# The first key piece as three transfers by partition modulo 4, and two small loads on GpSimd's queue

## The chip, the cores and the metric

The kernel runs on one core of one Trainium2 chip. The metric is the device time of one execution in microseconds (us), and the figure compared is the median over runs. Times inside an execution are counted from the start of the profiled span.

## The reference

One decode step for two sequences. A row `x` of 448 numbers per sequence is normalised; from it 16 query heads are projected, each attends to the last 4096 positions of a key and value cache (8 key/value heads, 256 wide, two query heads to one key head), and beside that a dense layer with a mish activation works on the same normalised row. The result is the sum of both and of `x`.

```python
def reference(A_x, A_k_cache, A_v_cache, A_wq, A_wo, B_x, B_w1, B_b1, B_w2):
    def _A_ref(x, k_cache, v_cache, wq, wo):
        W = min(4096, max(256, Sk // 4))
        rep = Hq // Hkv
        q = (x @ wq).reshape(B, Sq, Hq, Dh).transpose(0, 2, 1, 3)
        k = jnp.repeat(k_cache[:, :, Sk - W:, :], rep, axis=1)
        v = jnp.repeat(v_cache[:, :, Sk - W:, :], rep, axis=1)
        p = _softmax(jnp.einsum("bhqd,bhkd->bhqk", q, k) * (Dh ** -0.5), axis=-1)
        o = jnp.einsum("bhqk,bhkd->bhqd", p, v)
        return o.transpose(0, 2, 1, 3).reshape(B, Sq, Hq * Dh) @ wo
    def _B_ref(x, w1, b1, w2):
        h = jnp.einsum("bsd,df->bsf", x, w1) + b1
        sp = jnp.log1p(jnp.exp(-jnp.abs(h))) + jnp.where(h > 0, h, 0)
        return jnp.einsum("bsf,fd->bsd", h * jnp.tanh(sp), w2)
    xn = _layernorm(A_x, axis=-1)
    return A_x + _A_ref(xn, A_k_cache, A_v_cache, A_wq, A_wo) + _B_ref(xn, B_w1, B_b1, B_w2)
```

Everything is bf16. The keys and values that are read come to 67 MB, the weights to about 10 MB; the arithmetic on them is small.

## The kernel before

The eight key/value heads of the two sequences are taken in four steps `u` of four (sequence, head) pairs each; such a pair is called `j` below. A step needs two key pieces and two value pieces of 4 MB. All pieces, and the large weights `wq`, `w1` and `w2`, pass through a ring of three buffers of 128 partitions by 32 KB (`ring`, L87). A key piece (`load_k`, L92 to L99, its transfer L98) is laid out with partition p = 4c + j: c counts 32 stretches of the 4096 positions, j the four pairs, and every partition gets one run of 32 KB. So a piece is 128 runs, and all partitions with the same p modulo 4 hold one pair.

A key piece is turned by two VectorE transposes into `kt` (`turns`, L275), multiplied with the queries on TensorE (`scores`, L362), exponentiated on ScalarE (L370) and turned again on VectorE (L373). The value pieces are then multiplied by the weights (`values`, L408). Output projection and dense layer follow in the gaps, and the last step ends in the sum `acc` (L255), its copy to `res` (L626, L628) and the store (L629).

The order of work on every engine is the order in which the program is written, by hand (`tc.manual_schedule()`). SyncE (SP in the profile) issues nearly all transfers. Its queue begins with key piece (0,0) at L98, `wq` at L132 and key piece (0,1) at L98; these three fill the ring. The next issue, `w1` (L506), waits until `turns(0, 0)` has freed the first buffer, the next key piece waits until `project()` (L297) has used `wq`, and so on through the kernel. Ahead of it all ScalarE's queue issues two small loads, `x` (2 rows of 896 bytes, L126) and the bias `b1` (2 rows of 1792 bytes, L128). GpSimd (POOL) issues no transfer; its queue makes the identity matrix and then clears and fills constants: `qd` (L141), `ones`, `hot` (L151, L153), `xs` (L222) and `sp` (L287).

What hangs on `x`: VectorE's statistics (L162, L164), the normalised row (L171), its seven slices (L217), seven small transposes on TensorE (L218) and the copies into `xs` (L226). These stand in VectorE's queue ahead of `turns(0, 0)`, and between them stand constants that don't need `x` (L180 to L205). The bias is read first at L516, in the dense layer.

Of the kernel before, what the change touches and what calls it, by code (L numbers as in the profile page):

```python
# [17 lines left out]
def kernel(  # L18
# [13 lines left out]
    nc = tc.nc  # L32
    P = 128
    G = 4
    J = 4
    R = 4
    RK = 2
# [48 lines left out]
    KE = T * Dh  # L86
# [3 lines left out]
    def ring(name):  # L90
        return kv_pool.tile([P, RK * KE], BF16, tag="kv", name=name)

    k_t, v_t, wo_t = {}, {}, {}

    def load_k(u, r):
        t = ring("k")
        src = kview[u][:, s0:, :].rearrange("j (c t) d -> c j (t d)", c=C)
        nc.sync.dma_start(out=t[:], in_=src[:, :, r * RK * KE : (r + 1) * RK * KE])  # L98
        k_t[u, r] = t  # L99

    def load_v(u, g, lo=0, hi=TV):
# [8 lines left out]
    def load_wo(u):  # L110
# [12 lines left out]
        wo_t[u] = w  # L123

    x_bf = consts.tile([Bsz, D], BF16)
    nc.scalar.dma_start(out=x_bf[:, :], in_=A_x.flatten_outer_dims())  # L126
    b1_sb = consts.tile([2, F2], BF16)
    nc.scalar.dma_start(out=b1_sb[:], in_=B_b1.rearrange("(k f) -> k f", k=2))  # L128

    load_k(0, 0)  # L130
    wq = ring("wq")
    nc.sync.dma_start(  # L132
        out=wq[:, 0 : NS * HW], in_=A_wq.flatten().rearrange("(p e) -> p e", p=P)
    )
    wq_t = [wq[:, i * HW : (i + 1) * HW] for i in range(NS)]
    load_k(0, 1)

    ident = consts.tile([P, P], BF16)
    make_identity(nc, ident[:])
    qd = consts.tile([P, U, 2 * NB, G, NQ], BF16)  # L140
    nc.gpsimd.memset(qd[:], 0.0)  # L141
    ones = consts.tile([P, P], BF16)
# [3 lines left out]
        out=halves[:], in_=ident[0:2, 0:2].unsqueeze(2).to_broadcast([2, 2, Bsz])  # L146
# [5 lines left out]
    for k in range(KU):  # L152
        nc.gpsimd.tensor_copy(  # L153
            out=hot[:, k, :, :, :, k],
            in_=ident[:].rearrange("p (q y) -> p y q", y=4).unsqueeze(2)
# [11 lines left out]
        out=rstd[:], in_=mv[:, 1:2], func=ACT.Sqrt, bias=eps_t[:], scale=1.0  # L167
# [4 lines left out]
        out=xn_bf[:],  # L172
# [8 lines left out]
        out=parm[:], in_=ident[:].rearrange("p (a o) -> p o a", o=2), axis=AXIS.X, op=ALU.add  # L181
# [3 lines left out]
        out=jm[:],  # L185
        in_=ident[:].rearrange("p (a j h) -> p j a h", j=J, h=rep),
# [4 lines left out]
        out=jm[:], in0=jm[:], scalar1=-1.0, scalar2=29952.0, op0=ALU.add, op1=ALU.mult  # L191
# [3 lines left out]
        out=mneg[:], in_=jm[:].unsqueeze(1).to_broadcast([P, TH * 8, J])  # L195
    )
    sel = consts.tile([P, 2, NQ], FP32)
    for x in range(2):
        for w in range(4):
            at = 32 * w + (2 * (w % 2) + x) * NQ  # L200
            src = ident[:, at : at + NQ]
            if w == 0:
                nc.vector.tensor_copy(out=sel[:, x, :], in_=src)
            else:
                nc.vector.tensor_tensor(  # L205
                    out=sel[:, x, :], in0=sel[:, x, :], in1=src, op=ALU.add
# [4 lines left out]
    for s in range(NS):  # L211
        r = s // 2
        step = 3 + s % 2
# [9 lines left out]
    for odd in range(2):  # L223
        for half in range(2):
            o = (half + odd) % 2
            nc.vector.tensor_scalar(  # L226
                out=xs[:, odd::2, half * Bsz : (half + 1) * Bsz],
# [55 lines left out]
    for n in range(2):  # L283
        for e in range(2):
# [3 lines left out]
                out=sp[:],  # L288
                in_=ident[:, o : o + 63 : 2].unsqueeze(1).to_broadcast([P, G, 32]),
# [293 lines left out]
    for u in range(U - 1):  # L583
        load_k(u + 1, 0)
        load_v(u, 0)
        load_k(u + 1, 1)
        load_v(u, 1)
        load_wo(u)
        turns(u + 1, 0)
        values(u, 0)  # L590
        scores(u + 1, 0)
        turns(u + 1, 1)
        values(u, 1)
        gather(u)
        finish(u)
        scores(u + 1, 1)
        relay(u)
        mix_early(u)
        if u < U - 2:
            weigh(u + 1)  # L600
    u = U - 1
# [20 lines left out]
    for g in range(G):  # L622
        dst = res[:, g * DG : (g + 1) * DG]
        src = acc[32 * g : 32 * g + Bsz, :]
# [35 lines left out]
```

## Time and profile before

| what | us |
|---|---|
| median of 4 runs (lowest, highest) | 189.34 (189.28, 189.42) |
| the profiled execution's own time | 189.44 |
| its span in the profile | 187.6 |
| PE, VectorE, ScalarE, GpSimd busy | 74.1, 92.4, 12.4, 4.9 |
| first key piece, from issue to the transpose that waits for it | 0.73 to 13.39 |
| last weight transfer landed, last matmul group starts | 183.79, 183.84 |

The profiled execution is 0.10 us above the median, and 1.84 us of it lie outside the span. Busy times are of one execution; a transfer's row shows when its instruction was issued and how long the issue took, and not when its bytes moved. Stretches ("windows") give the mean busy share of the 16 DMA engines and the rate; a packet's whole time is put into the stretch in which it starts, so that shares over 1 stand next to shares under 1 where the stretches are short.

### The profile page before, as it was taken

Reading aid. Unit: us, or ns where it says so; the run is one execution under the profiler, and the core shown is the slowest. Engines: PE = TensorE matmul, PEld = TensorE weight load, DVE = VectorE, ACT = ScalarE, POOL = GpSimd, SP = SyncE. Lnnn points to the kernel's source line nnn. Section 1 sums busy time; section 2 is a strip of 40 time slices with the busy share of each in tenths; the row PEclk is TensorE's granted clock in tenths of the full one; section 3 lists DMA queues with packets and bytes.
Section 4 is the critical chain, followed back from the end, with each engine's and each line's share of the span. In section 5 each row is a group of like instructions: output and inputs, shape, how many; then the busy total and the mean of one; then the engine's idle time right before and its main releaser. Section 6 shows DMA issues by size and latency. Waiting matters only on the chain.

```text
span 187.6 us, 1952 instructions
## 1 busy us (share of the span) xinstructions
PE 74.1 (40%) x852; PEld 34.5 (18%) x856; DVE 92.4 (49%) x93; ACT 12.4 (7%) x26; POOL 4.9 (3%) x16
## 2 busy tenths in 40 slices
PE   0300367593119000882047002870068005854763
PEld 0100122451003000340012001430022002422452
DVE  6619724984891097038930395048910692040101
ACT  3000030101000100110001000110001000120101
POOL 8100000000000000000000000000000000000000
PEclk9999999999657955699559855798556655899555
DMA  6999999999999999999999999999999999999991
GB/s 225 433 421 428 430 433 406 475 444 433 419 412 430 426 449 387 472 447 433 440 412 409 440 440 418 449 437 447 433 426 412 426 433 433 433 416 398 432 406 40
DMA packets 4451, 77.78 MB, mean 415 GB/s; under 512 B 470, under 2 KB 1244, under 8 KB 2012
## 3 DMA queue, kind: packets, MB, share of 16 engines
q1 hardware_dynamic: 4436, 77.66, 96.8%
q8 instruction: 6, 0.10, 0.2%
q10 hardware_dynamic: 8, 0.01, 0.0%
q14 instruction: 1, 0.01, 0.0%
HBM read 77.67 MB, written 0.00 MB: 414 GB/s over the span
## 4 chain that ended last, share of the span: by engine, by line
DMA 57%; DVE 24%; PE 15%; ACT 2%; issue 1%; another core or an unknown queue 1%; SPq 0%; DVEq 0%
DMA v<-in_A_v_cache_dram 31%; DMA w<-in_B_w_dram 19%; DVE kt L275 19%; DMA k<-in_A_k_cache_dram 7%; PE pv L408 6%; PE sc L362 4%; DVE p L373 2%; PE h_ps L525 2%; PE o L426 1%; DVE rec L394 1%; ACT ex L370 1%; ACT vs L420 1%; PE acc L255 1%; DVE px L342 0%
## 5 line engine op out<-in xcount | busy, mean ns | idle before, releaser
L275 DVE STREAM_TRANSPOSE kt<-k 128x4096 f32<-128x4096 f32 x16 | 70.1, 4418 | 36.5 <-DMA k<-in_A_k_cache_dram 36.5
L408 PE MATMUL pv<-v,p 128*32 128x512 bf16 x240 | 24.3, 574 | 73.7 <-DMA v<-in_A_v_cache_dram 73.7
L408 PEld LDWEIGHTS <-p 128*32 128x32 bf16 x240 | 8.7, 130 | 86.4 <-issue 63.4
L362 PE MATMUL sc<-kt,qd 128*32 128x512 bf16 x256 | 20.1, 457 | 1.8 <-DVE qd L330 1.4
L453 DVE TENSOR_TENSOR oT<-o,rec 128x16 bf16<-128x16 f32 x4 | 0.7, 176 | 23.4 <-PE o L426 19.1
L373 DVE STREAM_TRANSPOSE p<-ex 128x512 bf16<-128x512 bf16 x8 | 5.2, 691 | 10.8 <-ACT ex L370 10.8
L370 ACT ACTIVATE ex<-sc 128x512 bf16<-128x512 f32 x8 | 4.8, 598 | 75.3 <-PE sc L362 75.3
L362 PEld LDWEIGHTS <-qd 128*32 128x32 bf16 x256 | 7.0, 107 | 12.3 <-issue 6.8
L297 PE MATMUL q_ps<-wq,xs 128*32 128x512 bf16 x28 | 3.2, 629 | 13.8 <-DMA wq<-in_A_wq_dram 13.8
L394 DVE TENSOR_REDUCE rec<-dn 128x8 f32<-128x512 f32 x4 | 2.8, 692 | 11.0 <-PE dn L386 9.6
L420 ACT COPY vs<-pv 128x512 f32<-128x512 f32 x4 | 2.3, 586 | 57.2 <-PE pv L408 57.2
L426 PE MATMUL o<-sel,vs 128*128 128x8 f32 x32 | 5.2, 289 | 2.1 <-ACT vs L420 2.1
L426 PEld LDWEIGHTS o<-sel,vs 128*128 128x128 f32 x32 | 4.8, 228 | 5.5 <-ACT vs L420 5.5
L487 PE MATMUL early<-wo,ox 128*2 128x448 bf16 x24 | 5.0, 352 | 1.9 <-ACT ox L478 1.9
L525 PE MATMUL h_ps<-xs,w 128*128 128x4 bf16 x49 | 3.7, 196 | 2.3 <-DMA w<-in_B_w_dram 2.3
L297 PEld LDWEIGHTS <-xs 128*32 128x32 bf16 x28 | 1.1, 136 | 15.5 <-issue 15.5
L386 PE MATMUL dn<-p,ones 128*128 128x512 bf16 x5 | 2.0, 433 | 4.1 <-DVE p L344 3.8
L218 PE MATMUL xr_ps<-ident,xrows 2*128 2x2 bf16 x7 | 1.0, 182 | 6.7 <-DVE xrows L217 6.7
L525 PEld LDWEIGHTS <-w 128*128 128x128 bf16 x49 | 3.2, 150 | 2.5 <-DMA w<-in_B_w_dram 2.4
L351 PE MATMUL sc<-mneg,ident 128*128 128x512 bf16 x7 | 3.1, 443 | 0.0
L441 PE MATMUL o<-p,v 128*128 128x8 bf16 x64 | 1.9, 168 | 1.7 <-DMA v<-in_A_v_cache_dram 1.7
L314 DVE COPY qT<-qt_ps 128x16 bf16<-128x16 bf16 x4 | 0.4, 167 | 4.3 <-PE qt_ps L309 4.3
(67 smaller groups left out, 43.9 us busy)
## 6 DMA issues: line engine op xcount, KB each, us to landing
k<-in_A_k_cache_dram SPq DMA_DIRECT2D x8, 4096.0 KB, 27.7
v<-in_A_v_cache_dram SPq DMA_DIRECT2D x7, 4096.0 KB, 21.3
wq<-in_A_wq_dram SPq DMA_DIRECT2D x1, 3584.0 KB, 20.4
wo<-in_A_wo_dram SPq DMA_DIRECT2D x3, 896.0 KB, 21.6
v<-in_A_v_cache_dram SPq DMA_DIRECT2D x1, 2048.0 KB, 17.7
w<-in_B_w_dram SPq DMA_DIRECT2D x1, 1568.0 KB, 13.1
v<-in_A_v_cache_dram SPq DMA_DIRECT2D x1, 1536.0 KB, 21.8
wo<-in_A_wo_dram SPq DMA_DIRECT2D x2, 448.0 KB
```

The lines of the kernel that those rows point to most:

```text
L275: nc.vector.transpose(out=kt[i][:, :, r, :, :], in_=t[:, r * KE : (r + 1) * KE].bitcast(FP32).rearrange("p (a c j) -> p a c j", c=P // (R ...
L297: nc.tensor.matmul(q_ps[32 * u : 32 * (u + 1), :], lhsT=xs[:, s, :], rhs=wq_t[s][:, u * 512 : (u + 1) * 512], start=(s == 0), stop=(s == N ...
L351: nc.tensor.matmul(sc[:].rearrange("p t c m -> p (t c m)"), lhsT=ident[:], rhs=mneg[:].rearrange("p a j -> p (a j)"), start=True, stop=Fal ...
L362: nc.tensor.matmul(sc[32 * w : 32 * (w + 1)].rearrange("p t c m -> p t (c m)"), lhsT=qd[:, u, 2 * n + e, :, :].rearrange("p g q -> p (g q) ...
L370: nc.scalar.activation(out=ex[:, :, :, i, :], in_=sc[:], func=ACT.Exp, scale=scale)
L373: nc.vector.transpose(out=p_all[:, :, h * TH : (h + 1) * TH, :].rearrange("p g t q -> p t g q"), in_=ex[:, h * TH : (h + 1) * TH].rearrang ...
L394: nc.vector.tensor_reduce(out=rec[:], in_=dn[:].rearrange("p a q -> p q a"), axis=AXIS.X, op=ALU.add)
L408: nc.tensor.matmul(pv[32 * w : 32 * (w + 1), :, :].rearrange("p x d -> p (x d)"), lhsT=p_run[:, g, 4 * a : 4 * a + 4, :].rearrange("p t q ...
L420: nc.scalar.copy(out=sb[:].rearrange("p x d -> p (x d)"), in_=pv[:].rearrange("p x d -> p (x d)"))
L426: nc.tensor.matmul(po[:, c, :], lhsT=sb[:, x, c::2], rhs=sel[:, x, :], start=(x == 0 and c == 0), stop=(last and x == 1), skip_group_check ...
L487: nc.tensor.matmul(early[:], lhsT=ox[:, i, :], rhs=w[:, i, :], start=False, stop=(u == U - 2 and i == 7),)
L525: nc.tensor.matmul(h_ps[:, i, :, :].rearrange("p k b -> p (k b)"), lhsT=w1_v[:, s, i, :], rhs=xs[:, s, 0 : 2 * Bsz], start=False, stop=(s ...
```

## The change

The function that loads a key piece takes a list of shares (first j, step). With the default it issues what it did before. For the first piece alone it is called with three shares: partitions 0, 4, 8, ... (32 runs), partitions 2, 6, 10, ... (32 runs), and the odd partitions (64 runs), each an issue of its own on SyncE's queue, into the same buffer. The loads of `x` and `b1` leave ScalarE's queue and are issued on GpSimd's, after the two instructions of the identity matrix and before the clearing of `qd`.

```diff
-    def load_k(u, r):
+    def load_k(u, r, shares=((0, 1),)):
         t = ring("k")
         src = kview[u][:, s0:, :].rearrange("j (c t) d -> c j (t d)", c=C)
-        nc.sync.dma_start(out=t[:], in_=src[:, :, r * RK * KE : (r + 1) * RK * KE])
+        for lo, step in shares:
+            nc.sync.dma_start(
+                out=t[lo:P:step, :], in_=src[:, lo:J:step, r * RK * KE : (r + 1) * RK * KE]
+            )
         k_t[u, r] = t
...
     x_bf = consts.tile([Bsz, D], BF16)
-    nc.scalar.dma_start(out=x_bf[:, :], in_=A_x.flatten_outer_dims())
     b1_sb = consts.tile([2, F2], BF16)
-    nc.scalar.dma_start(out=b1_sb[:], in_=B_b1.rearrange("(k f) -> k f", k=2))
-
-    load_k(0, 0)
+
+    load_k(0, 0, ((0, 4), (2, 4), (1, 2)))
     wq = ring("wq")
...
     make_identity(nc, ident[:])
+    nc.gpsimd.dma_start(out=x_bf[:, :], in_=A_x.flatten_outer_dims())
+    nc.gpsimd.dma_start(out=b1_sb[:], in_=B_b1.rearrange("(k f) -> k f", k=2))
     qd = consts.tile([P, U, 2 * NB, G, NQ], BF16)
```

## The prediction

> **What bounds the kernel.** I read the page's slices first, then the queue table, and then asked for stretches of time around the start.
>
> ```profile
> DMA  6999999999999999999999999999999999999991
> GB/s 225 433 421 428 430 433 406 475 444 433 419 412 430 426 449 387 472 447 433 440 412 409 440 440 418 449 437 447 433 426 412 426 433 433 433 416 398 432 406 40
> q1 hardware_dynamic: 4436, 77.66, 96.8%
> 13.40:180.00 166.60, 68.40 (x707) 30.34 (x712) 85.71 (x60) 10.36 (x22) 0.00 (x0) 0.76 1.00 431
> ```
>
> The 16 DMA engines are full in every slice but the first and the last, and at 431 GB/s over 166.6 us. 77.66 MB at that rate are 180.2 us of the 187.6 us span. So three things alone set the time: when the engines begin, whether they ever run dry or slow down, and what follows the last byte. The chain of waits names VectorE's transposes too (18.6%), but that is its way of walking through full buffers: where it waits longest, it waits for a transfer.
>
> Does the queue ever run dry? I add up the bytes issued on SP's queue at 431 GB/s and compare with the time of each later issue. The tightest is the value piece issued at 39.51: the bytes before it last until about 43.9, a reserve of 4.4 us. `w1` (issued 22.19) has about 8 us. The rows:
>
> ```profile
> 0.73 0.53 ACTq L126 DMA_DIRECT2D x_bf<-in_A_x_dram  x1
> 0.73 0.63 SPq L98 DMA_DIRECT2D k<-in_A_k_cache_dram  x1
> 1.29 0.24 ACTq L128 DMA_DIRECT2D b_sb<-in_B_b_dram  x1
> 1.42 0.57 SPq L132 DMA_DIRECT2D wq<-in_A_wq_dram  x1
> 2.05 0.62 DVE L162 BATCH_NORM_STATS2 stats<-x_bf 2x6 f32<-2x448 bf16 x1
> 2.05 0.54 SPq L98 DMA_DIRECT2D k<-in_A_k_cache_dram  x1
> ...
> 7.78 0.61 DVE L226 TENSOR_SCALAR xs<-xr_ps,parm 128x8 bf16<-128x8 bf16 x4 [0.36 <-PE xr_ps L218]
> 13.39 8.77 DVE L275 STREAM_TRANSPOSE kt<-k 128x4096 f32<-128x4096 f32 x2 [5.00 <-DMA k<-in_A_k_cache_dram]
> ...
> 22.19 0.34 SPq L506 DMA_DIRECT2D w<-in_B_w_dram  x1
> ...
> 39.51 0.54 SPq L106 DMA_DIRECT2D v<-in_A_v_cache_dram  x1
> ```
>
> They also show that VectorE idles 5.00 us before the first transpose. The start of the engines themselves, in stretches of the span (columns: stretch, its length, five engines' busy time, clock, DMA share, GB/s):
>
> ```profile
> 1.50:2.00 0.50, 0.00 (x0) 0.00 (x0) 0.50 (x2) 0.44 (x1) 0.50 (x1) 1.00 0.01 4
> 2.00:2.50 0.50, 0.00 (x0) 0.00 (x0) 0.50 (x4) 0.50 (x1) 0.50 (x3) 1.00 2.97 852
> 2.50:3.00 0.50, 0.00 (x0) 0.00 (x0) 0.33 (x2) 0.45 (x2) 0.50 (x1) 1.00 0.58 197
> 3.00:3.50 0.50, 0.00 (x0) 0.00 (x0) 0.24 (x2) 0.19 (x1) 0.44 (x2) 1.00 0.00 0
> ```
>
> 852 GB/s for 0.5 us are 426 KB, or 13 runs of 32 KB; 197 GB/s are 3 more. So the 16 engines take their first key run between 2.0 and 3.0, and none takes a second before 3.5. Their first runs fill (2.97 + 0.58) x 0.5 = 1.78 us per engine, against 1.22 us for a run in the steady part (32 KB at 431/16 = 26.9 GB/s). An engine thus counts as at full rate from about 2.3 + 1.78 - 1.22 = 2.9 us, some 2.1 us after SP's issue began at 0.73. This is what the change can reach. The single packets of the trace, which these stretches add up, start at 2.14 to 2.81.
>
> At the end nothing but bytes is waited for: the last weight lands at 183.79, and the last group of sums starts 0.05 us later.
>
> ```profile
> 183.84 1.09 PE L255 MATMUL acc<-w,act_bf 128*2 128x112 bf16 x28 [0.31 <-DMA w<-in_B_w_dram]
> ```
>
> The group before it waited for the same landings, so an earlier last byte is passed on whole.
>
> [...] the bias, issued by ACT, moved no byte until the first key runs were done (its packets start at 3.97 and 4.06). [...]
>
> **The change part by part.**
>
> (1) SP's first issue is a share of 32 runs. An issue with one source dimension less took 0.34 us (`w1`), the whole first piece 0.63: -0.29 us until the first descriptors are out, if form and company set the cost; zero if the first issue of an execution is dear by itself.
>
> (2) Each engine gets 2 runs with the first issue in place of 8. If the spread of the starts (2.14 to 2.81, 0.67 us) and the 0.56 us by which first runs are long come from writing out 128 runs for 16 engines, a quarter remains: up to -0.5 and -0.4 us. If they come from memory, nothing. I take -0.3 of the two together.
>
> (3) Two more issues on SP's queue, at most 0.63 us each by the row of the whole piece: `wq` goes out at about 2.7, the second key piece at about 3.3. Cover: the shares hold the engines until about 12. The first share alone lasts 2 x 1.22 = 2.4 us, the second is out by about 1.7. Cost nothing; without that cover, 0.6 us each. VectorE waits for three counts in place of one, nothing measurable.
>
> (4) `x` moves to GpSimd. Two identity instructions end at 1.30 (start 1.01, 0.29 long)[...]. Then its two rows queue behind a key run, and the completion behind another, as the bias' did: landing near 6 where it was before 2.05. What hangs on it took 2.05 to 8.39, 6.3 us, so `xs` is ready at about 12.3, still ahead of 13. Were it later, VectorE's queue holds `turns(0, 0)` behind it, and `w1`'s issue waits for that; the reserve there is 8 us, and `project()` needs `xs` only with `wq` at 21.97. Nothing to pay until `x` lands about 5 us later than this.
>
> (5) `b1` and GpSimd's memsets shift by 2 to 3 us. `b1` is read first at 32.77, `sp` at 27, `xs` is cleared well before 12. Nothing.
>
> (6) Small rows in the key stream. The bias' two rows took 0.50 and 0.60 us, each delaying one engine's key stream by that much. `x` went ahead of the keys (0.04 us); now it pays the same on two engines. If those are the ones that finish last, +0.5 us, otherwise nothing: 4 of 16 engines carry a small row afterwards instead of 2, so I take +0.15.
>
> Sum: -0.29 - 0.3 + 0.15 = -0.44 us. Against the profiled execution's 189.44 that is 189.0, and 188.9 against the median of 189.34, which I predict. Bounds: -1.2 to +0.5.
>
> **Rivals.** *It is hidden or not reached*: the start is set by memory's first answer, or a small row falls on the last engine and eats the gain. For it: first runs are long wherever they start. Time 189.3 (189.0 to 189.7).
>
> *The shares lose the engines' rate* (the other side). With 128 partitions every run takes 1.22 us[...]. [...] A run then takes up to 2.44 us; eight of them add 8 x 1.22 = 9.8 us, 199; if a quarter of them collide, +2.4 - 0.44, 191.3. It decides once the first piece's runs average about 9% longer than 1.22 (8 x 0.11 = 0.85 us turns -0.44 into +0.4). [...] For it: nothing here shows such a share.
>
> *The shares wait for each other*: three writers of one buffer. If each waits for the one before to land, the engines empty twice, each time from the last byte (0.3 us to the count, as for `k` before, then 1.6 us from issue to full rate): 2 x 1.9 - 0.5 = +3.3, 192.6. Against it: two parts of one value piece go out at 157.74 and 158.33 with no wait between, though those are ranges of columns.
>
> **Chances.** Earlier start shows: 0.44, nearly all of it beyond -0.38 us. Hidden: 0.24. Rate lost: 0.19. Shares wait: 0.07. Small rows on the last engines with no gain in start, about 189.9: 0.06. About 0.2%, or 0.38 us, is what a measurement of this kernel can tell from no change; with that faster 0.41, same 0.27, slower 0.32. The first two cases lie within 188.4 and 189.7 and hold two thirds; up to 192.8 the last two and the milder half of the lost rate come in. The likeliest case's own range is 188.4 to 189.2.
>
> **What would show it.** Right: a first SP issue near 0.34 us; 16 first runs starting within 1.6 to 2.2; the first piece landed by about 12.9; `w1`'s issue earlier, all later landings earlier by the same 0.3 to 0.6 us. Part (4) is wrong if the idle time before the first transpose names anything but the key transfer. Rate lost: the stretch from 5 to 13 well under 431 GB/s. Shares waiting: gaps between the three issues at L98. The forecast fails most easily through what no row shows, the dealing out of a strided share.

## The result and the profile after

The changed kernel takes 189.69 us (median of 31 runs, 189.36 to 190.05) against 189.42 us (49 runs of the kernel before on the same chip, 189.06 to 189.91). The ratio is 1.0016, 95% interval 1.0011 to 1.0021: about 0.3 us slower, clear of noise, though inside the 0.2% that the prediction called no change. The forecast was 0.44 us faster. One execution of the kernel called e6 below took 210.11 us, in the slower state that executions sometimes fall into, and its ratio leaves it out.

The page after, its slices and its queue table (q0 is GpSimd's queue, and ScalarE's q10 is gone):

```profile
DMA  6999999999999999999999999999999999999990
GB/s 223 448 419 391 447 419 424 477 443 441 412 398 433 436 447 388 477 440 447 440 412 401 433 440 424 441 447 443 440 433 419 412 420 438 433 426 395 431 402 29
q1 hardware_dynamic: 4468, 77.66, 96.8%
q0 software_dynamic: 64, 0.01, 0.0%
```

The bytes are the same and the engines are as full as before. The same stretches as in the prediction (stretch, length, five engines' busy time, clock, DMA share, GB/s):

```profile
2.00:2.50 0.50, 0.00 (x0) 0.00 (x0) 0.00 (x0) 0.02 (x1) 0.50 (x2) 1.00 3.19 852
2.50:3.00 0.50, 0.00 (x0) 0.00 (x0) 0.00 (x0) 0.00 (x0) 0.50 (x2) 1.00 0.56 197
3.00:3.50 0.50, 0.00 (x0) 0.00 (x0) 0.00 (x0) 0.00 (x0) 0.50 (x2) 1.00 0.00 0
13.40:180.00 166.60, 72.94 (x702) 32.12 (x707) 85.59 (x60) 10.35 (x22) 0.00 (x0) 0.71 1.00 431
```

Again 13 first runs start between 2.0 and 2.5 and 3 between 2.5 and 3.0. They fill (3.19 + 0.56) x 0.5 = 1.88 us per engine, where it was 1.78. So the first runs became longer, not shorter. The steady rate is 431 GB/s as before. SyncE's issues around the start, then GpSimd's, then VectorE's rows:

```profile
0.74 1.85 SPq L99 DMA_DIRECT2D k<-in_A_k_cache_dram  x3
2.64 0.70 SPq L133 DMA_DIRECT2D wq<-in_A_wq_dram  x1
3.38 0.63 SPq L99 DMA_DIRECT2D k<-in_A_k_cache_dram  x1
...
1.45 0.65 POOL L141 DMA_DIRECT2D x_bf<-in_A_x_dram  x1
2.09 0.52 POOL L142 DMA_DIRECT2D b_sb<-in_B_b_dram  x1
...
7.22 0.61 DVE L165 BATCH_NORM_STATS2 stats<-x_bf 2x6 f32<-2x448 bf16 x1 [5.65 <-DMA x_bf<-in_A_x_dram]
...
12.68 0.61 DVE L229 TENSOR_SCALAR xs<-xr_ps,parm 128x8 bf16<-128x8 bf16 x4 [0.36 <-PE xr_ps L221]
13.40 8.77 DVE L278 STREAM_TRANSPOSE kt<-k 128x4096 f32<-128x4096 f32 x2
```

The three shares go out back to back (0.74 to 2.59). VectorE starts on `x` at 7.22 in place of 2.05, and the idle time before the first transpose has gone: it follows the last copy into `xs`.

The end has to be read anew. `w2` comes in four pieces, and these are the last three in the list of transfers of the kernel before (size, us from issue to landing), with the store of the kernel before and of the changed one:

```profile
w<-in_B_w_dram SPq DMA_DIRECT2D x1, 448.0 KB, 22.9
w<-in_B_w_dram SPq DMA_DIRECT2D x1, 224.0 KB, 15.5
w<-in_B_w_dram SPq DMA_DIRECT2D x1, 112.0 KB, 10.9
...
185.58 0.34 SPq L629 DMA_DIRECT2D out_dram<-res  x1
...
185.74 0.32 SPq L632 DMA_DIRECT2D out_dram<-res  x1
```

By the completion records they land at 183.79, 184.36 and 184.62. So the 183.79 that is called the last weight ahead of the prediction and in it is the landing of the 448 KB piece; the sums that start at 183.84 are followed by others that wait for the two smaller pieces, the last from 184.67 on. The last weight lands at 184.62 in the kernel before and at 184.78 in the changed one, and in both the store goes out 0.96 us later. An earlier or later last byte is passed on whole, as the prediction said. The spans differ by 0.23 us (187.56 and 187.79 by the trace): 0.16 us of this are the last weight, and most of the rest lies after the store. One profile can't carry tenths, though: a second profile of the changed kernel (e12 below) has its last weight at 184.51. So I use the ratios of all executions for sizes and the records for places.

### The profile page after: what moved, and what is told of

Same layout as the page of the kernel before. It is cut to its first block, busy times and chain, and to the rows that moved or that the text cites. A ratio compares the mean times of both kernels' runs of the same rounds, so it can differ in the third digit from the quotient of the medians.

```text
span 187.8 us, 1957 instructions
## 1 busy us (share of the span) xinstructions
PE 78.9 (42%) x852; PEld 36.4 (19%) x856; DVE 91.5 (49%) x93; ACT 12.4 (7%) x26; POOL 5.8 (3%) x18
## 4 chain that ended last, share of the span: by engine, by line
DMA 51%; DVE 26%; PE 17%; ACT 2%; issue 1%; another core or an unknown queue 1%; POOL 0%; DVEq 0%; SPq 0%; POOLq 0%
DMA v<-in_A_v_cache_dram 29%; DMA w<-in_B_w_dram 19%; DVE kt L278 18%; PE pv L411 6%; PE sc L365 5%; DMA x_bf<-in_A_x_dram 3%; DVE p L376 2%; PE o L429 2%; PE h_ps L528 2%; DVE rec L397 1%; ACT ex L373 1%; ACT vs L423 1%; PE acc L258 1%; DVE sel L208 1%
## 5 line engine op out<-in xcount | busy, mean ns | idle before, releaser
L365 PE MATMUL sc<-kt,qd 128*32 128x512 bf16 x256 | 21.9, 493 | 2.0 <-DVE qd L333 1.6
L429 PE MATMUL o<-sel,vs 128*128 128x8 f32 x32 | 6.7, 339 | 2.3 <-ACT vs L423 2.3
L429 PEld LDWEIGHTS o<-sel,vs 128*128 128x128 f32 x32 | 6.4, 293 | 5.5 <-ACT vs L423 5.5
L354 PE MATMUL sc<-mneg,ident 128*128 128x512 bf16 x7 | 4.0, 566 | 0.0
L165 DVE BATCH_NORM_STATS2 stats<-x_bf 2x6 f32<-2x448 bf16 x1 | 0.6, 615 | 5.7 <-DMA x_bf<-in_A_x_dram 5.7
```

The lines of the kernel that those rows point to most:

```text
L354: nc.tensor.matmul(sc[:].rearrange("p t c m -> p (t c m)"), lhsT=ident[:], rhs=mneg[:].rearrange("p a j -> p (a j)"), start=True, stop=Fal ...
L365: nc.tensor.matmul(sc[32 * w : 32 * (w + 1)].rearrange("p t c m -> p t (c m)"), lhsT=qd[:, u, 2 * n + e, :, :].rearrange("p g q -> p (g q) ...
L429: nc.tensor.matmul(po[:, c, :], lhsT=sb[:, x, c::2], rhs=sel[:, x, :], start=(x == 0 and c == 0), stop=(last and x == 1), skip_group_check ...
```

## The experiments

The trace also has 16 completion records for each large transfer, which I take as one per DMA engine; each of the three shares of the changed kernel has 16 too. From them I take the mean over the 16 engines (how far the stream of bytes is) and the last (what a waiting engine sees); "close" is from the store's last completion to the end of the span. All times in us; ratios are to the kernel before on the same chip, from all executions, so that they can differ a little from the quotients of the medians. The median of the kernel before was 189.39 to 189.42 on all of them.

| kernel | median | ratio (95%) | first piece landed, mean / last | store issued | close |
|---|---|---|---|---|---|
| before | 189.42 | | 13.00 / 13.37 | 185.58 | 0.84 |
| changed | 189.69 | 1.0016 (1.0011 to 1.0021) | 13.05 / 13.27 | 185.74 | 0.90 |
| e12, changed again | 189.66 | 1.0017 (1.0009 to 1.0024) | 13.02 / 13.62 | 185.47 | 0.90 |
| e1, split only | 189.76 | 1.0015 (1.0009 to 1.0022) | 13.02 / 13.38 | 185.69 | 1.00 |
| e2, GpSimd only | 189.63 | 1.0010 (1.0003 to 1.0016) | 12.92 / 13.12 | 185.49 | 1.02 |
| e11, GpSimd, two more issues | 189.55 | 1.0011 (1.0004 to 1.0017) | 13.02 / 13.29 | 185.73 | 0.90 |
| e4, bias on SyncE | 189.29 | 0.9998 (0.9989 to 1.0006) | 12.92 / 13.18 | 185.46 | 0.83 |
| e10, e4 and two more issues | 189.52 | 1.0007 (0.9999 to 1.0015) | 12.89 / 13.15 | 185.55 | 1.00 |
| e9, e4 and split | 189.65 | 1.0015 (1.0009 to 1.0022) | 12.98 / 13.35 | 185.64 | 1.00 |
| e9b, the same again | 189.72 | 1.0018 (1.0010 to 1.0026) | 12.98 / 13.45 | 185.92 | 1.00 |
| e8, e4, second issue late | 189.41 | 0.9999 (0.9991 to 1.0008) | 12.91 / 13.17 | 185.49 | 0.83 |
| e5, all key pieces split | 190.17 | 1.0042 (1.0028 to 1.0055) | 12.98 / 13.29 | 185.60 | 1.34 |
| e3, first 4 KB first | 190.44 | 1.0049 (1.0035 to 1.0063) | 13.66 / 14.44 | 186.90 | 0.94 |
| e6, two halves | 199.55 | 1.0528 (1.0512 to 1.0544) | 22.98 / 23.55 | 195.67 | 0.93 |

### The parts alone

**e1, split only.** The first piece in three shares, `x` and the bias on ScalarE's queue.

```diff
     x_bf = consts.tile([Bsz, D], BF16)
+    nc.scalar.dma_start(out=x_bf[:, :], in_=A_x.flatten_outer_dims())
     b1_sb = consts.tile([2, F2], BF16)
+    nc.scalar.dma_start(out=b1_sb[:], in_=B_b1.rearrange("(k f) -> k f", k=2))
...
-    nc.gpsimd.dma_start(out=x_bf[:, :], in_=A_x.flatten_outer_dims())
-    nc.gpsimd.dma_start(out=b1_sb[:], in_=B_b1.rearrange("(k f) -> k f", k=2))
```

(to the changed kernel)

> The first key piece in three shares, x and the bias on ScalarE's queue as before. Theory A (the share gains nothing at the start and costs almost nothing; the changed kernel's loss comes with GpSimd's queue, in closing the program and in x): within 0.1 us of before. Theory B (the shares cost: longer first runs and two more completions on every engine hold all later bytes back): 0.2 to 0.3 us over before, the whole loss of the changed kernel. If the share did start the engines earlier and x or the bias ate it: 0.2 to 0.4 us under before. The first of the three issues should take near 0.57 us, as in the changed kernel.

**e2, GpSimd only.** To the changed kernel:

```diff
-    load_k(0, 0, ((0, 4), (2, 4), (1, 2)))
+    load_k(0, 0)
```

> The first key piece whole, x and the bias on GpSimd's queue. Theory A: 0.2 to 0.3 us over before, the whole loss, with the close of the program (store landed to end of span) some 0.06 us longer and xs ready only at about 13. Theory B: within 0.1 us of before.

Measured: e1 1.0015, e2 1.0010, which is 0.28 us (0.17 to 0.42) and 0.19 us (0.06 to 0.30). Each part alone loses; theory A had expected it of e2 only, theory B of e1 only. Together they would make 0.47 us, where the changed kernel has 0.30 (0.21 to 0.40). The intervals don't tell these two apart, but the table shows a reason why the parts need not add: both e1 and e2 have a close of 1.0, and the changed kernel has 0.90.

The reason for the close is seen in SP's own instructions. After the store SP waits for one completion count after the other (in the kernel before from 185.97 on, the first four 0.06 us apart), and every wait that stands behind the store's takes 0.06 us. In the changed kernel, as in the one before, the store's count is the last of the list. The traces show eight counts, used by the issues of SyncE and ScalarE in turn, and with two issues more on SP's queue (e1) or two fewer (e2) the store's count moves ahead, so that three or two waits follow its landing. In the changed kernel two issues left ScalarE's queue and two came to SP's, and the list ends with the store again; what stays there is 0.06 us, most of it GpSimd's clearing of the counts (0.139 in place of 0.096 us).

e2 also tests the prediction's part (4). Its VectorE rows:

```profile
8.27 0.62 DVE L165 BATCH_NORM_STATS2 stats<-x_bf 2x6 f32<-2x448 bf16 x1 [6.71 <-DMA x_bf<-in_A_x_dram]
13.73 0.61 DVE L229 TENSOR_SCALAR xs<-xr_ps,parm 128x8 bf16<-128x8 bf16 x4 [0.36 <-PE xr_ps L221]
14.26 8.76 DVE L278 STREAM_TRANSPOSE kt<-k 128x4096 f32<-128x4096 f32 x2
```

Here `x` is so late that the transposes start 1.1 us after the piece has landed (13.12), and `w1` is issued at 23.04 in place of 22.19. The last weight still lands at 184.53, no later than before (184.62): the reserve on SP's queue takes it, as the prediction had it. Nearly all of e2's loss, 0.18 of 0.19 us, is its longer close.

### What sets the start

**e3, the first 4 KB first.** To the kernel before:

```diff
-        nc.sync.dma_start(out=t[:], in_=src[:, :, r * RK * KE : (r + 1) * RK * KE])
+        edges = (0, *cuts, RK * KE)
+        for lo, hi in zip(edges, edges[1:]):
+            nc.sync.dma_start(
+                out=t[:, lo:hi], in_=src[:, :, r * RK * KE + lo : r * RK * KE + hi]
+            )
...
-    load_k(0, 0)
+    load_k(0, 0, (2048,))
```

> As before, but the first piece comes as the first 4 KB of each of the 128 runs and then the other 28 KB, two issues. If the 1.4 us from issue to first byte and the 0.56 us by which first runs are long are the answer time of memory and queue, whatever the size: first bytes again at about 2.1 and the time within 0.1 us of before. If they grow with the bytes or runs of the first issue: first bytes at 1.7 or so, and up to 0.4 us under before.

Measured 1.0049, slower by 0.9 us; neither side expected it. The stretches:

```profile
2.00:2.50 0.50, 0.00 (x0) 0.00 (x0) 0.50 (x3) 0.50 (x1) 0.50 (x3) 1.00 0.67 172
2.50:3.00 0.50, 0.00 (x0) 0.00 (x0) 0.50 (x3) 0.34 (x1) 0.50 (x1) 1.00 1.77 279
3.00:3.50 0.50, 0.00 (x0) 0.00 (x0) 0.43 (x5) 0.00 (x0) 0.44 (x2) 1.00 0.38 65
3.50:4.00 0.50, 0.00 (x0) 0.00 (x0) 0.15 (x1) 0.29 (x1) 0.50 (x2) 1.00 1.00 328
```

The first packet starts at 2.17, as with 32 KB (2.14). The first packets take 0.16 to 0.4 us, and then, from 2.4 to 3.0, some packets of the same 4 KB start that take 0.8 to 1.3 us; the last of these ends at 3.9, and from then on most take 0.16 us. So there is a stall of this length near the start with runs of 4 KB too. It lies where the first runs of 32 KB lie, which fits that these are long because of it. What it is, e3 doesn't tell: its first issue also has 128 runs. With short runs the last engine comes out of it 1 us behind the mean (the first share's last completion at 5.99, its mean at 4.97). Both the mean and the spread stay: the first piece lands 0.66 us later on average, and the last transfer 0.68 us later on average and 1.32 us later on its last engine.

**e4, the bias on SyncE's queue.** To the kernel before:

```diff
-    nc.scalar.dma_start(out=b1_sb[:], in_=B_b1.rearrange("(k f) -> k f", k=2))
...
     load_k(0, 1)
+    nc.sync.dma_start(out=b1_sb[:], in_=B_b1.rearrange("(k f) -> k f", k=2))
```

> As before, but the bias is issued on SyncE's queue behind the second key piece. Its two rows then no longer stand between the first and second key runs of two engines, where they took 0.5 and 0.6 us. If these two engines finish last: 0.3 to 0.5 us under before. If the engines that finish last are others (those that fetch instructions late in the kernel, by the changed kernel's trace): within 0.1 us of before, while the first piece's last landing comes earlier.

Measured 0.9998, the second case. The first piece's mean landing is 0.08 us earlier (two rows of 0.5 and 0.6 us over 16 engines make 0.07), the time is not measurably changed. This is the best of all versions run, and it is not told apart from the kernel before.

**e8, the second issue late.** To e4: the load of `wq` and what follows on SP's queue move behind the reciprocal, after a VectorE write into the same buffer.

```diff
     wq = ring("wq")
+    nc.vector.memset(wq[:, 0:1], 0.0)
     nc.sync.dma_start(
         out=wq[:, 0 : NS * HW], in_=A_wq.flatten().rearrange("(p e) -> p e", p=P)
     )
```

(The lines are shown where they now stand; `load_k(0, 1)` and the bias follow them.)

> As the kernel with the bias on SyncE's queue, but the second issue (wq) waits for a VectorE write at about 3.4 us, so that no issue runs beside the first key runs. If the issues of 1.4 to 2.6 us make the first runs long (1.8 in place of 1.21 us): first runs near 1.3 us and 0.3 to 0.5 us under the kernel with the bias on SyncE's queue. If memory's first answer does: first runs of 1.7 to 1.9 us again and the same time within 0.1 us.

```profile
0.73 0.63 SPq L98 DMA_DIRECT2D k<-in_A_k_cache_dram  x1
4.05 0.35 SPq L165 DMA_DIRECT2D wq<-in_A_wq_dram  x1
```

```profile
2.00:2.50 0.50, 0.00 (x0) 0.00 (x0) 0.50 (x3) 0.50 (x1) 0.50 (x3) 1.00 2.70 786
2.50:3.00 0.50, 0.00 (x0) 0.00 (x0) 0.50 (x3) 0.08 (x1) 0.50 (x1) 1.00 0.73 262
```

With SP silent from 1.4 to 4.0 the first runs still take (2.70 + 0.73) x 0.5 = 1.72 us. The issues of `wq` and of the second key piece beside them are not the cause. `wq` went out 2.6 us later, and the ratio is 0.9999 against e4's 0.9998, which confirms the cover of part (3).

### What a share does to the rate

**e6, two halves.** To e1: two shares by partitions 0 to 63 and 64 to 127.

```diff
-    def load_k(u, r, shares=((0, 1),)):
+    def load_k(u, r, shares=1):
...
-        for lo, step in shares:
-            nc.sync.dma_start(
-                out=t[lo:P:step, :], in_=src[:, lo:J:step, r * RK * KE : (r + 1) * RK * KE]
-            )
+        for lo in range(0, C, C // shares):
+            hi = lo + C // shares
+            nc.sync.dma_start(
+                out=t[lo * J : hi * J, :], in_=src[lo:hi, :, r * RK * KE : (r + 1) * RK * KE]
+            )
...
-    load_k(0, 0, ((0, 4), (2, 4), (1, 2)))
+    load_k(0, 0, 2)
```

> x and the bias on ScalarE's queue as before; the first piece in two shares by partitions 0 to 63 and 64 to 127[...]. The prediction's rival of a share [...]: runs of up to 2.4 us in the first piece, its landing up to 9.7 us later, the time up to 199. [...]

```profile
5.00:13.40 8.40, 1.45 (x8) 0.77 (x8) 3.27 (x21) 0.00 (x0) 0.31 (x2) 1.00 0.98 207
13.40:23.00 9.60, 0.00 (x0) 0.00 (x0) 0.00 (x0) 0.00 (x0) 0.00 (x0) 1.00 0.94 212
23.00:180.00 157.00, 64.26 (x655) 27.58 (x662) 84.97 (x58) 9.77 (x21) 0.00 (x0) 0.74 1.00 431
```

While the halves are loaded all 16 engines are busy (shares of 0.98 and 0.94) and move 207 to 212 GB/s, half of 431; each run takes 2.5 us. The time is 199.55, where the prediction's rival of a lost rate had 199; its runs of twice the length were an assumption that no row of before shows. So such a loss exists, and the strided shares escape it: in the changed kernel the runs after the first take 1.21 to 1.25 us on average. Why a block of 64 partitions runs at half the rate, no trace shows.

**e5, all key pieces split.** To e1:

```diff
-    def load_k(u, r, shares=((0, 1),)):
+    def load_k(u, r, shares=((0, 4), (2, 4), (1, 2))):
```

> x and the bias on ScalarE's queue as before, and all eight key pieces in three shares, with the store's completion on the same place among the closing waits as before. If a share costs bytes or completions on the engines wherever it stands [...]: seven more split pieces add seven times what one adds, 0.3 us or more, and the rate in the steady part falls under 431 GB/s. If the split of the first piece costs only at the start (longer first runs): no more than 0.1 to 0.2 us over before, at 431 GB/s.

Measured 1.0042, slower by 0.8 us, which looks like the first case. The profile says otherwise:

```profile
13.40:180.00 166.60, 70.25 (x708) 30.35 (x713) 85.90 (x60) 10.35 (x22) 0.00 (x0) 0.73 1.00 431
...
185.60 0.34 SPq L632 DMA_DIRECT2D out_dram<-res  x1
```

The rate is 431 GB/s, and the store is issued at 185.60, where it was 185.58 before. In this profile seven more split pieces cost the bytes nothing. What is seen of the loss comes after the store: close 1.34 in place of 0.84 us, because SP goes on 0.45 us after its last wait, at 187.30, and not at once. What holds SP there the records don't name. The queue table shows one instruction transfer more than before (q14: 2 for 1), but it starts at 187.92, too late to be the cause. The other 0.3 us of the 0.8 are not placed: the profiled execution was the shortest of the five.

### What the split and the queue cost

**e9, split with the bias on SyncE's queue,** and **e10, the piece whole but as many issues.** e9 is e4 with the three shares of the change; e10 is e4 with

```diff
-    nc.sync.dma_start(out=b1_sb[:], in_=B_b1.rearrange("(k f) -> k f", k=2))
+    b1_in = B_b1.rearrange("(k f) -> k f", k=2)
+    for lo, hi in ((0, 300), (300, 600), (600, F2)):
+        nc.sync.dma_start(out=b1_sb[:, lo:hi], in_=b1_in[:, lo:hi])
```

> The first piece in three shares, x on ScalarE's queue, the bias on SyncE's behind the second key piece: the split alone, with no small rows among the key runs. Against the kernel with the bias on SyncE's queue and the piece whole: if the split costs at the start, the mean landing of the first piece 0.1 us later and the last weight 0.1 to 0.2 later; in time 0.2 to 0.35 over it, since the store's completion moves ahead in the closing waits too (three more waits of 0.065 behind it). If the split gains once the small rows are gone: the first piece's mean landing earlier.

> As the kernel with the bias on SyncE's queue, with the bias in three issues of some 300 columns: two more issues and completions than there, the first key piece whole. If the number of SP's issues moves the store's completion ahead in the closing waits and that costs by itself: about 0.17 us over the kernel with the bias in one issue (close 0.99 in place of 0.83 us), the store issued at the same time. If the closing waits cost nothing: the same time. Its difference to the split with the same number of issues is what the split costs on the bytes: 0.1 to 0.2 us by the theory that the start pays, zero by the theory that only the close does.

> The first piece in three shares, x on ScalarE's queue, the bias on SyncE's, a second time and on the chip of the kernel with two more issues: 0.1 to 0.2 us over that one if the start pays, the same if only the close does.

e10 changes nothing but the number of issues and goes from 0.9998 to 1.0007, 0.17 us; its close is 0.17 us longer, as expected. Who waited for whom on SP's queue at the end, in e4 and then in e10 (total, times, longest):

```profile
SPq L655 <- DMA out_dram<-res: 0.6, 1, 0.6
```

```profile
SPq L657 <- DMA out_dram<-res: 0.8, 1, 0.8
```

In e4 this wait is the last of the list; in e10 it is the second, begins earlier and is followed by three more. The place and the size in the trace agree with the difference of the ratios; but the two intervals overlap, and that of e10 just reaches 1, so the price in time is probable and not beyond doubt.

e9 and e9b, with the same number of issues as e10, are 0.15 and 0.21 us above it by the ratios; the intervals overlap a little. Their first piece lands 0.08 us later on average and 0.20 and 0.30 us later on its last engine. At the end the average no longer shows it: the last weight's mean completion is at 183.60 and 183.59, where e4 and e10 have 183.52 and 183.73. Its last completion does, at 184.68 and 184.96 against 184.51 and 184.59.

**e11, GpSimd's queue with the changed kernel's number of issues.** To e2:

```diff
-    nc.sync.dma_start(
-        out=wq[:, 0 : NS * HW], in_=A_wq.flatten().rearrange("(p e) -> p e", p=P)
-    )
+    wq_in = A_wq.flatten().rearrange("(p e) -> p e", p=P)
+    for lo, hi in ((0, 5 * HW), (5 * HW, 6 * HW), (6 * HW, NS * HW)):
+        nc.sync.dma_start(out=wq[:, lo:hi], in_=wq_in[:, lo:hi])
```

> x and the bias on GpSimd's queue, the first piece whole, and wq in three issues by columns: as many issues on SP as in the changed kernel, so that the store's completion comes last as there. Close near 0.90 us in place of the 1.02 of the kernel with GpSimd alone, the store issued 0.1 us earlier than before; time within 0.1 us of before, and 0.15 to 0.3 us under the changed kernel if the split pays at the start.

**e12** is the changed kernel again.

> The changed kernel on the chip of the three others: 0.2 to 0.4 us over before; close near 0.90 us, the rest on the bytes.

e11 has the close that was expected (0.90). Its time was not: 1.0011 is 0.21 us over before (0.08 to 0.32), and the store went out at 185.73, not earlier than before. The two runs of the changed kernel have 1.0016 and 1.0017, as expected of e12. So most of the loss stays with a whole first piece, and the shares add about 0.1 us, which the intervals don't tell from zero.

e11 is not GpSimd's queue alone, though. It also cuts `wq` into three issues, at 1.43 to 2.51 us, beside the first key runs. Its first runs end at 4.16 on average and its first piece lands at 13.02, as in the kernels with a split piece and unlike e2 (4.07 and 12.92). More issues beside the first key runs may be what these kernels have in common, rather than the shares or GpSimd's queue. A run with `wq` cut in three and `x` and the bias on ScalarE's queue would tell; there is none. The length of the first runs also varies: it is 1.88 and 1.80 us in two profiles of the changed kernel.

## Why the prediction was wrong

**The step that failed is the earlier start, parts (1) and (2), -0.59 us of the sum.** The engines did not come to full rate earlier. Over all profiles but e3 and e6 the first key runs end at 4.11 to 4.19 us on average over the engines in the six with a split piece, and at 4.07 to 4.16 in the six with a whole one; the averages of these are 4.15 and 4.10. Without the two parts the prediction's own sum is +0.15 us. That this lies near the measured 0.3 is luck, for it is part (6), and that was wrong too.

**Part (1), -0.29 us.** It took 0.34 us for an issue of 32 runs from the row of `w1`, issued at 22.19. The first share took 0.57 us in place of 0.63, the second 0.58, the third 0.60. The prediction's rows held a warning: `wq` has no more source dimensions than `w1`, and its issue at 1.42 took 0.57 us. In e8, where it goes out at 4.05, it took 0.35. So the stage of the program counts. The form does too: in e5 the first shares of the later pieces, of the same form as here, still take 0.48 to 0.52 us. The rest of the reasoning was not refuted. By the single packets, the first key packet starts 0.77 to 0.80 us after the end of SP's first issue in all fourteen profiles, and with the issue shorter by 0.06 us it came at 2.10 in place of 2.14. But this gain was lost again by the end of the first runs.

**Part (2), -0.3 us.** It offered two readings of the spread of the starts and of the long first runs, writing out 128 runs or memory's answer, and took the middle. Nothing of it came: the starts are spread over 0.58 us in the changed kernel and 0.72 in e12 (0.67 before), and the first runs take 1.88 and 1.80 us (1.78 before). Which reading holds stays open. e8 excludes other issues beside the first runs, and e3 shows the stall with short runs; but both have 128 runs in the first issue, and in the changed kernel the other 96 follow within 1.9 us. A first share of 32 runs with nothing behind it until 4 us was not run. Why the shares end a little later, and more spread, stays open too.

**Part (3) held for the bytes.** The second and third large loads went out at 2.64 and 3.38, and the rate from 5 us on is that of before. What it left out is the close: the number of issues decides where the store's completion stands in the last list of waits, 0.17 us for the wrong place in the profiles (e4 against e10). In this change the count happened to come out even.

**Part (4) held in its price and not in its time.** GpSimd's issue took 0.65 us (1.45 to 2.09), but `x` had landed at 7.2 for an estimate of 6, and `xs` was ready at 13.29 for 12.3, later than the first piece's landing at 13.27. So the margin that the prediction saw ("still ahead of 13") was used up, and the key transfer no longer ends any idle time before the first transpose, which was its sign against this part. It cost nothing all the same, since the transposes start at 13.40 for 13.39 before; and e2, where they start at 14.26, shows that the reserve on SP's queue takes more than that. **Part (5)** shows no cost of its own: the first of GpSimd's memsets that stand behind its issues shifts by 1.36 us (2.60 for 1.24).

**Part (6) had the wrong price and sign.** The rows of `x` and the bias took 0.04 and 0.07 us in the changed kernel, not 0.5, and the bias' 0.5 and 0.6 us went away. That is a gain of 0.06 us on average over the engines (0.08 in e4, which takes the bias away from there altogether), worth nothing measurable in time.

**What the loss consists of** is known in part. 0.06 us are the longer close, seen in both profiles of the changed kernel and in e11. The other 0.2 us or so can't be divided with certainty. For the shares, four comparisons point the same way, none of them well clear of noise by itself: e1 against before (0.12 us beside its close), e9 against e4 (0.15 beside its close), e9b against e10 (0.21), the changed kernel against e11 (about 0.1). For GpSimd's queue, which the prediction gave no price beside its rows, e2 leaves next to nothing beside its close and e11 leaves 0.15 us, with the cut of `wq` in it.

Of the rivals, "hidden or not reached" came true in its time, at the edge of its range (189.0 to 189.7), though not with a loss on top. "Shares wait for each other" is refuted by the three issues from 0.74 to 2.59. "The shares lose the engines' rate" is refuted for these shares (430 GB/s from 5 to 13.4 us in the changed kernel) and shown for two blocks of 64 partitions (207 and 212).

## What to carry to other kernels

When a kernel's DMA engines are full from the first byte to the last, look at three places only: the first byte, the slowest engine, and the end of the program. Before pricing a smaller first transfer, look for an issue of its form at the same stage of the program, and ask when the first runs end and not only when the first byte comes. If a tile must be loaded in shares, stride the partitions as here (429 to 436 GB/s); two blocks of 64 neighbours ran at 207 to 212.

## What the runs showed that I had not expected

- Two blocks of 64 partitions ran at 207 to 212 GB/s, strided shares of 32, 32 and 64 at 429 to 436.
- Near the start packets of 4 KB stall for 0.8 to 1.3 us, between 2.4 and 3.9 us; loading the first piece so cost 0.9 us of the whole time, about half of it on all engines and half through the spread between them (e3).
- Where the store's completion stands in the closing list of waits is worth 0.06 us for each wait behind it. With 16 issues more on SP's queue SP also went on 0.45 us late after the last wait (e5, one profile).
- Two profiles of one kernel differ by 0.27 us in the last weight's last completion (184.78 and 184.51) while its mean over the engines agrees to 0.02 us (183.64 and 183.62): it is the slowest engine that varies.
- The slowest engines lag by more than all that this change is about. In the kernel before ten engines complete the last weight by 183.44, one at 183.76 and five at 184.22 to 184.62. Up to 31.54 us no engine lagged by more than 0.37 us behind the median. After that instruction transfers of 16 KB come at 39.1, 60.9, 100.8, 126.0 and 165.8 (queue q8, about 0.9 us each), and after each of them one engine more lags by over 0.8 us: one, 1.24 us late, after the first, and five at the end; a sixth transfer comes at 182.9, when the first engines complete the last weight (182.87). This fits that each of them holds up one engine's stream for good. No run moved or removed one.
